# One of every five attention transposes moves from the DMA queue to TensorE

## The chip, the cores and the metric

The kernel runs on one core of a Trainium2 chip. Its time is the device time in microseconds (us) of one execution. Before the change the median of three runs was 1784.25 us (1779.7 to 1787.0). An engine here is one of TensorE (PE in the profile, with its weight loads as PEld), VectorE (DVE), ScalarE (ACT), GpSimd (POOL) and SyncE (SP), which only issues transfers.

## The reference

The program computes an attention with a position bias and feeds it to a mixture of eight experts whose gate is balanced by eight rounds of row and column normalisation. Batch 4, 8 heads, 576 positions, head size 64; 2304 tokens, model width 512, hidden width 1024.

```
scores = q @ k.T / sqrt(64) + bias            # 4 x 8 x 576 x 576
attn   = exp(scores - max);  attn /= sum + 1e-9
x      = (attn @ v), heads side by side       # 2304 x 512
P      = exp(x @ w_gate - max), 8 x (rows to 1, columns to 1, times N/E)
out    = sum over 8 experts e of P[:, e] * (relu(x @ w1[e]) @ w2[e])
```

## The kernel before

Every fp32 matrix is held as a pair of fp16 matrices, a high part and a low remainder, and products are formed from such pairs.

**The attention** works in 16 units, one for each pair of heads of each batch (`units`, line 687). The 576 queries of one head are cut into tiles of 128 rows: four full ones, and a half tile of 64; the half tiles of the two heads of a unit share the fifth tile. A unit has five steps (`unit_steps`, line 1086): for `gi` 0 and 1, one step per head with two tiles each, and for `gi` 2 one step with the fifth tile alone. A tile passes through these stages: `st_scores` (PE, into a PSUM tile `s`), `st_max` (DVE, adds the bias and takes the maximum, gives `sb`), `st_exp` (ACT), `st_rcp` (DVE), `st_hi` (ACT writes the high half of the probabilities into `ah`), `st_lo` (DVE writes the low half). `ah` has two buffers, and holds 2 x 576 numbers for each tile of a step. The probabilities must then be transposed so that the keys lie on the partitions: nine blocks of 128 x 128 for one tile (4.5 high, 4.5 low), eighteen for a step with two tiles. Line 975 does it with one transposing DMA on the SP queue, from `ah` to `aT` (three buffers for eighteen blocks; the fifth tile has one buffer of its own, `aT4`, printed as aT in the trace). Two steps later `attend` (line 977) multiplies `aT` with the values on PE, into PSUM tile `pv`, and `fin` writes the result as a high and a low half.

The same stretch of time also holds other work. The first 130 us or so compute the bias. All units load q, k, v and bias tiles (`nat`, `bt`) on the same SP queue, and split and transpose q and k: `u_trans` (line 753) transposes 18 blocks of `qk` on PE with `id16` as the moving operand, into a PSUM tile `l1`, from which ACT copies eight and two blocks and DVE eight. The first expert's products (`run_piece`, line 870, PSUM tiles `l1` and `l2`) are filled in between at lower priority.

The PSUM tile `s` has two buffers of 1024 fp32 columns each, that is two banks of 2048 bytes per partition. `ps_s` (line 449) hands them out in turn.

**What sets the order.** The instructions are not issued as they are written. `Plan` (line 43) collects them with their operands, finds what depends on what, and lays them out by a list scheduling with assumed costs (`cost`, `transfer`); each engine then runs its own list strictly in that order. So a new instruction can shift all that follows it in the attention. The experts 1 to 7 come after a first `plan.emit` (line 1185), in a plan of their own.

Of the kernel before, what the change touches and what calls it, by code (L numbers as in the profile page):

```python
# [9 lines left out]
F16 = mybir.dt.float16  # L10
# [8 lines left out]
P = 128  # L19
# [251 lines left out]
def attention_sinkhorn_moe(ctx, tc, q, k, v, w1, b1, w2, wg, m1, m2, xm, xm4, xf, sel, out):  # L271
# [11 lines left out]
    plan = Plan()  # L283
    vec, act, pool, pe, sync = (
        Engine(plan, e, n)
        for e, n in ((nc.vector, "dve"), (nc.scalar, "act"), (nc.gpsimd, "pool"), (nc.tensor, "pe"), (nc.sync, "dma"))
    )
# [15 lines left out]
    id16 = consts.tile([P, P], F16, name="id16")  # L303
# [109 lines left out]
    with ExitStack() as actx:  # L413
# [35 lines left out]
        def ps_s():  # L449
            return psA.tile([P, 1024], F32, name="ps_s", tag="s", bufs=2)  # L450
# [68 lines left out]
        for kind in range(1, 4):  # L519
            vec.scalar_tensor_tensor(  # L520
                out=wr,
# [8 lines left out]
            out=wa.rearrange("p g (j k) -> p (g j) k", j=4),  # L530
# [92 lines left out]
        def bias_step(between=()):  # L623
# [27 lines left out]
            out=w1r, in0=pw[:, H : H + 2], scalar1=s_wb[:, 0:1], scalar2=2.0**-11, op0=ALU.mult, op1=ALU.mult  # L651
# [5 lines left out]
            out=w2m,  # L657
# [22 lines left out]
        for i in range(2):  # L680
            r = slice(32 * i, 32 * i + 1)
# [113 lines left out]
        for n in range(8):  # L795
            for m in (2 * n, 2 * n + 1):
                nm, _, i = qk_order[m]
# [9 lines left out]
        with plan.urgent():  # L807
# [6 lines left out]
            out=c8, in0=u_qk[:, 0:1], scalar=0.125, in1=u_qk[:, 1:2], op0=ALU.mult, op1=ALU.mult  # L814
# [7 lines left out]
            out=g, in0=g0, scalar=s_qk[:, 0:1], in1=s_qk[:, 1:2], op0=ALU.mult, op1=ALU.mult  # L822
# [140 lines left out]
        def st_lo(s):  # L963
            n, ah = len(s["sb"]), s["ah"]
            s["aT"] = wrk.tile([P, 9 * n, P], F16, name="aT", tag="aT" if n == 2 else "aT4", bufs=3 if n == 2 else 1)
            for i, sb in enumerate(s["sb"]):
                vec.scalar_tensor_tensor(
                    out=ah[:, i, S:],
                    in0=sb,
                    scalar=s["st"][:, 3, i : i + 1],  # L970
                    in1=ah[:, i, 0:S],
                    op0=ALU.mult,
                    op1=ALU.subtract,
                )
            sync.dma_start_transpose(out=s["aT"], in_=ah.rearrange("p n s -> p (n s)"))

        def attend(u, gi, ss):

# [158 lines left out]
        for n in range(NS + LAG + 1):  # L1137
# [19 lines left out]
            if 0 < n <= NS:  # L1157
                s = steps[n - 1]
                st_hi(s)
                st_lo(s)  # L1160
                u, gi, hh = s["key"]
                groups.setdefault((u, gi), []).append(s)
                if gi == 2 or hh == 1:
                    due.append((n + LAG, u, gi, groups.pop((u, gi))))
# [21 lines left out]
        vec, act, pool, pe, sync = nc.vector, nc.scalar, nc.gpsimd, nc.tensor, nc.sync  # L1186
# [682 lines left out]
    for n, (e, b) in enumerate(seq):  # L1869
        r = visit[n]  # L1870
        i, at_end, leaves = (b, r % 2), n % 5 == 4, visit[n + 1 : n + 2] != [r]
# [96 lines left out]
```

## Time and profile before

| | us |
|---|---|
| median of 3 runs (range) | 1784.25 (1779.7 to 1787.0) |
| the profiled execution | 1784.56 |
| its span in the trace | 1782.8 |
| around the span | 1.76 |
| attention units with five steps each, steady stretch | 258 to 488 |
| last attention products | about 516.7 |

The profiled execution is 0.31 us above the median. Line L210 is the helper in which every planned instruction is recorded, so the attention is read by the names of the tiles. `l` stands for the PSUM tiles l1 and l2, `id` for the identity matrix, `area` for a large SBUF area that holds the first expert's weights at that time, `xc` and `xb` for the attention's output. The share of the DMA engines is the mean over the core's 16 engines.

How the views below are read. A row of the windows has the stretch and its length, then the busy time of PE, PEld, DVE, ACT and POOL with the number of instructions, then TensorE's granted clock (1.00 is its upper level), the share of the DMA engines and GB/s. A row of the waits says who waited for whom, and then the total in us, how often, and the longest. A row of the timeline has the start, the duration, the engine, the line, the operation and how many instructions were merged; the merged span begins with the first and ends with the last. A row of the chain has the start and the length of one piece. A group of instructions has its number, then the busy time of all in us and the mean duration of one in ns (instructions that overlap count once in the busy time), and then the idle time of its engine just before and who ended it.

### The profile page before, as it was taken

The numbers are of one execution on the slowest core, as the hardware profiler recorded it, in microseconds if no ns is written. First come the engines' busy times: TensorE is split into PE (matmuls) and PEld (weight loads), VectorE is DVE, ScalarE is ACT, GpSimd is POOL, SyncE is SP. The second block draws the span as 40 slices with busy tenths as digits, with TensorE's granted clock in tenths as the row PEclk, the third lists the DMA queues.
The fourth block names the chain that finished last, engine by engine and source line by source line (L and its number), as shares of the span: only waits on it lengthen the run. The fifth ranks groups of instructions, "written<-read, shape, count | busy, mean of one in ns | idle before, by whom it ended". The sixth has DMA issues, their size and how long they took to land.

```text
span 1782.8 us, 40479 instructions
## 1 busy us (share of the span) xinstructions
PE 1686.8 (95%) x16640; PEld 1377.4 (77%) x16640; DVE 1447.8 (81%) x2627; ACT 1086.3 (61%) x1930; POOL 78.7 (4%) x90
## 2 busy tenths in 40 slices
PE   7887897898989999999999999999999999999998
PEld 4544564555666688888988898889888988898887
DVE  6898988898968898778887787878788878876666
ACT  7887888888856675545564555565555544453443
POOL 0120012122200000000000000000000000000000
PEclk9988799999999999999999999999999999999999
DMA  7769999999993164644473557445545653463321
GB/s 259 240 160 225 206 196 200 200 201 194 202 268 136 68 204 181 231 165 163 170 279 135 201 190 248 154 143 213 214 173 180 237 192 131 160 238 103 104 73 37
DMA packets 303358, 324.24 MB, mean 182 GB/s; under 512 B 191420, under 2 KB 231876, under 8 KB 298180
## 3 DMA queue, kind: packets, MB, share of 16 engines
q1 hardware_dynamic: 303172, 321.65, 60.0%
q8 instruction: 130, 2.13, 0.5%
q14 instruction: 56, 0.46, 0.1%
HBM read 189.86 MB, written 88.08 MB: 156 GB/s over the span
## 4 chain that ended last, share of the span: by engine, by line
PE 78%; DVE 8%; DMA 7%; ACT 3%; issue 2%; SPq 0%; DVEq 0%; ACTq 0%
PE bankA L1591 18%; PE bankA L1611 13%; PE bankE L1591 9%; PE bankE L1611 9%; PE bankB L1611 9%; PE l L210 6%; PE bankB L1591 4%; DMA aT<-ah 4%; PE s L210 4%; PE pv L210 3%; ACT area L210 2%; DVE ah L210 1%; DVE area L210 1%; DVE sb L210 1%; PE bankS L1427 1%
## 5 line engine op out<-in xcount | busy, mean ns | idle before, releaser
L1591 PEld LDWEIGHTS <-slot 128*128 128x128 f16 x5040 | 450.7, 98 | 48.3 <-issue 2.5
L1611 PEld LDWEIGHTS <-hA 128*128 128x128 f16 x2268 | 222.4, 98 | 27.1 <-issue 0.6
L210 PEld LDWEIGHTS <-area 128*128 128x128 f16 (+1 forms) x2477 | 155.2, 101 | 101.5 <-issue 33.2
L1591 PE MATMUL bankA<-xt,slot 128*128 128x256 f16 (+1 forms) x1680 | 186.1, 262 | 0.2 <-ACT u L1648 0.2
L1591 PE MATMUL bankE<-xt,slot 128*128 128x256 f16 (+1 forms) x1680 | 186.1, 262 | 0.0
L1636 ACT ACTIVATE hA<-c 128x512 f16<-128x512 f32 x189 | 118.0, 627 | 111.3 <-DVE c L1214 110.4
L1611 PEld LDWEIGHTS <-hS 128*128 128x128 f16 x1512 | 147.2, 98 | 22.2 <-ACT hS L1636 3.0
L1611 PEld LDWEIGHTS <-area 128*128 128x128 f16 x1512 | 148.0, 98 | 18.5 <-issue 1.4
L210 DVE SCALAR_TENSOR_TENSOR ah<-sb,st,ah 128x576 f16<-128x576 f32 x144 | 122.4, 876 | 24.1 <-ACT ah L210 23.9
L1214 DVE SCALAR_TENSOR_TENSOR hA<-c,hA 128x512 f16<-128x512 f32 x189 | 127.5, 685 | 12.3 <-ACT hA L1636 10.2
L1695 ACT COPY u<-bankA 128x512 f32<-128x512 f32 (+1 forms) x70 | 37.8, 540 | 157.6 <-PE bankA L1611 157.4
L210 ACT ACTIVATE ah<-sb,st 128x576 f16<-128x576 f32 x144 | 106.2, 770 | 37.6 <-DMA aT<-ah 33.5
L1648 ACT ACTIVATE u<-bankA 128x512 f32<-128x512 f32 x126 | 75.1, 596 | 67.6 <-PE bankA L1591 63.8
L210 ACT ACTIVATE sb<-sb,st 128x576 f32<-128x576 f32 x144 | 110.4, 769 | 7.4 <-DVE st L210 7.1
L210 PE MATMUL l<-area 128*128 128x512 f16 (+1 forms) x413 | 110.6, 385 | 3.5 <-ACT ys L210 0.4
L1214 DVE SCALAR_TENSOR_TENSOR acc<-c,fs,acc 128x256 f32<-128x256 f32 x252 | 110.6, 480 | 2.1 <-DMA out_dram<-acc 0.2
L210 PE MATMUL s<-qkT 128*128 128x512 f16 (+3 forms) x560 | 84.5, 302 | 23.0 <-DVE st L210 22.1
L1611 PE MATMUL bankA<-area,hS 128*128 128x256 f16 x756 | 88.6, 273 | 3.2 <-ACT hS L1636 2.5
L1611 PE MATMUL bankA<-area,hA 128*128 128x256 f16 x756 | 89.8, 276 | 0.0
L1611 PE MATMUL bankA<-area 128*128 128x256 f16 x756 | 88.2, 273 | 1.0 <-ACT u L1695 1.0
L1611 PE MATMUL bankE<-area,hS 128*128 128x256 f16 x756 | 88.5, 273 | 0.0
L1611 PE MATMUL bankB<-area,hA 128*128 128x256 f16 x756 | 88.2, 273 | 0.0
(239 smaller groups left out, 3155.6 us busy)
## 6 DMA issues: line engine op xcount, KB each, us to landing
sc_w<-stage SPq DMA_DIRECT2D x84, 512.0 KB
acc<-sc_y SPq DMA_DIRECT2D x102, 256.0 KB
area<-sc_w SPq DMA_DIRECT2D x48, 512.0 KB
sc_y<-acc SPq DMA_DIRECT2D x84, 256.0 KB
xt<-sc_t SPq DMA_DIRECT2D x18, 1024.0 KB
slot<-sc_w SPq DMA_DIRECT2D x36, 512.0 KB
bt<-sc_bias SPq DMA_DIRECT2D x26, 576.0 KB
raw<-in_moe_w_dram SPq DMA_DIRECT2D x28, 512.0 KB
```

The lines of the kernel that those rows point to most:

```text
L210: self.plan.record(self.name, cost, lambda: fn(*args, **kw), ins, outs, move)
L1214: vec.scalar_tensor_tensor(out=o, in0=x, scalar=s, in1=y, op0=op0, op1=op1)
L1427: pe.matmul(r, id16 if sg > 0 else nid16, v[:, a, 2 * dq : 2 * dq + 2, tok * w : tok * w + w], start=(j == 0), stop=(j == len(seq_) - 1),)
L1591: pe.matmul(ps[:, jf * w : jf * w + w], t[:, a, c * 512 + f * P : c * 512 + f * P + P], x(xp, c), start=(first and jf == 0 and c == 0 and ...
L1611: pe.matmul(ps[:, j * 256 : j * 256 + 256], h[:, a, fc * w + j * P : fc * w + j * P + P], t[:, wp, fc * 256 : fc * 256 + 256], start=(firs ...
L1636: on_act(0.58, lambda: act.activation(h[:, 0, sl], x, AF.Relu if relu else AF.Copy), [r], wk)
L1648: on_act(0.55, lambda: act.activation(tmp[k], bank[b], f, scale=HS), [b], [k], 0)
L1695: on_act(0.27 * nt, lambda: act.copy(tmp[k][:, :n], bank[b][:, :n]), [b], [k], 0)
```

## The change

For the step with the fifth tile (`gi` 2) no transposing DMA is issued any more. Instead a tile of the `s` ring is taken, read as fp16, and nine blocks of `ah` are transposed into it on PE, as one piece for the planner. ACT then copies blocks 0 to 4 (640 columns) to `aT4`, DVE blocks 5 to 8 (512 columns). The other four steps of a unit keep their DMA.

```
@@ -972,7 +972,17 @@  st_lo
-            sync.dma_start_transpose(out=s["aT"], in_=ah.rearrange("p n s -> p (n s)"))
+            u, gi, hh = s["key"]
+            if not (gi == 2):
+                sync.dma_start_transpose(out=s["aT"], in_=ah.rearrange("p n s -> p (n s)"))
+                return
+            for i in range(n):
+                ps = ps_s().bitcast(F16)[:, : 9 * P].rearrange("p (r x) -> p r x", x=P)
+                with plan.as_one():
+                    for r in range(9):
+                        pe.transpose(ps[:, r], ah[:, i, r * P : (r + 1) * P], id16)
+                act.copy(s["aT"][:, 9 * i : 9 * i + 5], ps[:, :5])
+                vec.tensor_copy(s["aT"][:, 9 * i + 5 : 9 * i + 9], ps[:, 5:])
```

In all 16 transfers go, and 144 block transposes, 16 copies of ACT and 16 of DVE come. Apart from the lines of the source, the lists of all engines are the same from the end of the attention on. Within it the planner lays out everything after the first fifth tile anew.

On the SP queue, near the end of the attention, the order before is this (the number before the bracket is the shape; `DMAHW` are completion counters of earlier transfers):

```order
L210 DMA bt_1_123<-sc_bias_70 128x1152 [waits DMAHW6_49,DVE_49]
L210 DMA_TRANSPOSE aT_1_124<-ah_1_144 128x18x128 [waits DMAHW7_49,DVE_49,PE_49]
L210 DMA_TRANSPOSE aT_2_138<-ah_0_142 128x18x128 [waits DMAHW0_49,DVE_49,PE_49]
L210 DMA_TRANSPOSE aT_0_122<-ah_1_144 128x18x128 [waits DMAHW1_49,DMAHW5_49,DVE_49,PE_49]
L210 DMA_TRANSPOSE aT4_0_117<-ah_0_142 128x9x128 [waits DMAHW2_49,DVE_49]
L210 DMA_TRANSPOSE aT_1_124<-ah_1_144 128x18x128 [waits DMAHW3_49,DMAHW7_49,DVE_49,PE_49]
```

And now, in the same place:

```order
L210 DMA_TRANSPOSE aT_0_122<-ah_0_142 128x18x128 [waits DMAHW1_49,DVE_49,PE_49]
L210 DMA_TRANSPOSE aT_1_124<-ah_1_144 128x18x128 [waits DMAHW0_49,DMAHW3_49,DVE_49,PE_49]
L210 DMA bt_1_123<-sc_bias_70 128x1152
L210 DMA_TRANSPOSE aT_2_138<-ah_0_142 128x18x128 [waits DMAHW2_49,DMAHW4_49,DVE_49,PE_49]
L210 DMA_TRANSPOSE aT_0_122<-ah_1_144 128x18x128 [waits DMAHW7_49,DVE_49,PE_49]
```

The nine-block transfer between the large ones is gone; the large ones now follow each other directly, with only loads between them.

On PE, in the thirteenth unit, the scores of one step end and the q and k blocks of a later unit follow. Before (`s_0` and `s_1` are the two buffers of the scores' PSUM tile):

```order
L210 LDWEIGHTS qkT_1_129
L210 MATMUL s_1_118<-qkT_1_129 128x512 [waits DVE_49]
...
L210 MATMUL s_1_118<-qkT_1_129 128x64
L210 LDWEIGHTS qk_0_125
L210 MATMUL l1_1_115<-id16_68,qk_0_125 128x128 [waits DVE_49]
```

And now:

```order
L210 MATMUL s_1_118<-qkT_1_129 128x512 [waits DVE_49]
...
L210 LDWEIGHTS ah_0_142 [waits Activation_49]
L210 MATMUL s_0_116<-id16_68,ah_0_142 128x128
...
L210 LDWEIGHTS ah_0_142 [waits DVE_49]
...
L210 LDWEIGHTS qk_0_125
L210 MATMUL l1_1_115<-id16_68,qk_0_125 128x128 [waits DVE_49]
...
L210 MATMUL s_0_116<-qkT_1_129 128x512 [waits Activation_49]
```

Nine transposes stand between, four behind a wait for ACT's half of `ah` and five behind one for DVE's half; the next scores into `s_0` wait for ACT's copy.

On ACT the same place reads before as follows (`sb` in and out is `st_exp`, into `ah` is `st_hi`):

```order
L210 ACTIVATE sb_5_141,st_1_135<-sb_5_141,st_1_135 128x576
L210 ACTIVATE sb_0_133,st_1_135<-sb_0_133,st_1_135 128x576 [waits DVE_49]
L210 COPY qkT_0_126<-l1_0_113 128x1024 [waits PE_49,Pool_49]
L210 ACTIVATE ah_1_144<-sb_3_137,st_0_132 128x576 [waits DMAHW4_49,DVE_49]
L210 ACTIVATE ah_1_144<-sb_4_140,st_0_132 128x576
```

And now:

```order
L210 ACTIVATE sb_5_141,st_1_135<-sb_5_141,st_1_135 128x576
L210 ACTIVATE sb_0_133,st_1_135<-sb_0_133,st_1_135 128x576 [waits DVE_49]
L210 COPY aT4_0_117<-s_0_116 128x640 [waits DVE_49]
L210 ACTIVATE ah_1_144<-sb_3_137,st_0_132 128x576 [waits DMAHW2_49]
L210 ACTIVATE ah_1_144<-sb_4_140,st_0_132 128x576
L210 COPY qkT_0_126<-l1_0_113 128x1024 [waits Pool_49]
```

The new copy stands ahead of `st_hi` of the next step, and what it waits for is DVE's copy of the other four blocks. DVE's copy waits for PE's transposes, and ACT's for DVE's: the two do not run side by side. That is so in 12 of the 16 units; in the other four DVE's copy waits for ACT's.

## Rows read from the trace of the kernel before

**Rows 1.** The page: busy us, then PE and the DMA in 40 slices, tenths.

```profile
PE 1686.8 (95%) x16640; PEld 1377.4 (77%) x16640; DVE 1447.8 (81%) x2627; ACT 1086.3 (61%) x1930; POOL 78.7 (4%) x90
...
PE   7887897898989999999999999999999999999998
...
DMA  7769999999993164644473557445545653463321
```

**Rows 2.** Windows: a stretch of the attention, one of the experts.

```profile
258.00:488.00 230.00, 203.07 (x2027) 130.19 (x2025) 203.91 (x452) 192.04 (x389) 49.49 (x50) 0.97 0.96 200
700.00:1700.00 1000.00, 994.89 (x9557) 892.12 (x9555) 796.89 (x1294) 521.09 (x859) 0.00 (x0) 1.00 0.51 181
```

**Rows 3.** Waits, 186 to 509 us: the four that bear on this.

```profile
ACT ah L210 <- DMA aT<-ah: 26.2, 24, 2.2
DVE ah L210 <- ACT ah L210: 23.9, 23, 2.5
PE s L210 <- DVE st L210: 21.7, 27, 2.1
PE pv L210 <- DMA aT<-ah: 7.5, 9, 2.6
```

**Rows 4.** Chain of waits, 150 to 520 us, shares by line.

```profile
by line: PE l L210 25.1%; DMA aT<-ah 20.7%; PE pv L210 13.0%; PE s L210 9.2%; DVE ah L210 6.3%; issue 5.1%; DVE sb L210 3.8%; DVE area L210 2.4%; ACT ah L210 2.0%; DMA area<-in_moe_w_dram 1.5%; DVE sms L210 1.2%; DVE qk L210 1.2%; ACT sb L2
```

**Rows 5.** Timeline of the SP queue in one unit.

```profile
412.07 3.68 SPq L210 DMA_TRANSPOSE aT<-ah  x1
415.80 1.26 SPq L210 DMA_DIRECT2D nat<-in_q_dram  x2
417.17 3.28 SPq L210 DMA_TRANSPOSE aT<-ah  x1
420.54 0.53 SPq L210 DMA_DIRECT2D sc_y<-ys  x1
421.17 1.33 SPq L210 DMA_TRANSPOSE aT<-ah  x1
422.59 0.52 SPq L210 DMA_DIRECT2D bt<-sc_bias  x1
```

**Rows 6.** The same timeline: two nine-block transfers, four units apart.

```profile
258.01 1.25 SPq L210 DMA_TRANSPOSE aT<-ah  x1
...
351.11 1.39 SPq L210 DMA_TRANSPOSE aT<-ah  x1
```

**Rows 7.** Chain of waits, 409 to 425 us: one passage through a transpose.

```profile
414.97 2.20 PE l L210 x15
417.17 4.85 DMA aT<-ah
422.02 0.04 issue
422.06 1.93 PE pv L210 x27
```

**Rows 8.** Groups of instructions by form, 150 to 520 us.

```profile
L210 PE MATMUL l<-id,qk 128*128 128x128 f16 x216 | 18.1, 224 | 2.9 <-DVE area L210 1.8 <-ACT qkT L210 0.6 <-DVE qk L210 0.2
L210 ACT COPY qkT<-l 128x1024 f16<-128x1024 f16 x12 | 12.0, 1003 | 2.8 <-PE l L210 2.6 <-issue 0.2
L210 DVE COPY qkT<-l 128x1024 f16<-128x1024 f16 x12 | 8.2, 686 | 2.1 <-PE l L210 1.8
L210 ACT COPY qkT<-l 128x256 f16<-128x256 f16 x12 | 4.3, 358 | 0.9 <-PE l L210 0.9
```

**Rows 9.** Timeline: eight block transposes of TensorE in a row.

```profile
413.86 0.62 PE L210 MATMUL l<-id,qk 128*128 128x128 f16 x8
```

**Rows 10.** Waits in the tail of the attention, 486 to 512 us.

```profile
DVE ah L210 <- ACT ah L210: 7.1, 4, 2.5
ACT ah L210 <- DMA aT<-ah: 5.3, 4, 2.2
```

## The prediction

> **What bounds the kernel now.** I read the page first, for where the span goes. TensorE is busy 95% of it, and in the slices it is at 9 from the thirteenth on, but for the last; the DMA engines fill their slices from the fourth to the twelfth and not after [rows 1]. The windows say the same in numbers: from 700 to 1700 us PE is busy 994.89 of 1000 us with the DMA at 0.51, and that part keeps its order. So the change acts only on the attention, and what it wins or loses there moves the rest as a block.
>
> In the steady stretch of the attention, 258 to 488 us, four resources are nearly level: PE 203.07 of 230 us (88.3%), DVE 203.91 (88.7%), ACT 192.04 (83.5%), and the DMA engines at 0.96 [rows 2]. The fullest one is the DMA. The waits show how it is felt: ACT waits for a transfer out of `ah` to end (24 times, 26.2 us), because a buffer of `ah` is free only when its transpose has landed; DVE then waits for ACT's half of `ah` (23 times, 23.9 us); PE waits for `aT` itself only 7.5 us, and 21.7 us for DVE to release a scores tile [rows 3]. The chain of waits gives the weights: of 370 us, PE's three lines hold 47.3% (25.1 + 13.0 + 9.2), the transposing transfers 20.7%, that is 77 us, and DVE's named lines some 15% [rows 4]. One passage of the chain through an eighteen-block transfer takes 4.85 us, of which its 3.28 us on the queue are the larger part [rows 5, 7].
>
> **What goes.** Sixteen nine-block transfers. One holds the SP queue for 1.25 to 1.39 us, 1.33 in the middle; an eighteen-block one for 3.28 to 3.68 us, so that half of it, up to 1.85, is the other bound [rows 5, 6]. In all 21 to 30 us of a queue that is nearly always full, about 1.3 to 1.85 us in a unit. A unit is 23.3 us long (from the nine-block transfer at 258.01 us to the fourth one after it, at 351.11, divided by four [rows 6]), so the DMA's 0.96 would fall to about 0.89. What this frees is bounded by what is now waited for the transposes: 26.2 us (ACT) and 7.5 us (PE), 33.7 together [rows 3]. Below, nothing may come back, since four eighteen-block transfers in each unit remain and each still has to land before its buffer is free; it could even cost, as the planner lays out all transfers anew and two large ones now stand next to each other on the queue. I take half of the 33.7, about 17, and of that nine tenths, since 23.9 of ACT's 26.2 us were handed on to DVE: 15 us. The tail speaks for a real share: from 486 to 512 us, where little else is left to do, ACT waits 5.3 us for transposes and DVE 7.1 us for ACT [rows 10].
>
> **What comes on PE.** 144 block transposes, nine in a unit. The same form exists for q and k: 216 of them keep PE busy 18.1 us, 84 ns each, though one alone lasts 224 ns, because they overlap [rows 8]; eight in a row end within 0.62 us [rows 9]. So 9 x 84 = 0.76 us in a unit, 12.1 us in all; at the other end, without any overlap, 9 x 224 = 2.0 us, 32 us in all. I take 12.1, since these too stand in a row. PE has idle time in the stretch, 27 of 230 us, and its work is on the chain for 47.3% of it; 12.1 x 0.47 = 5.7 us.
>
> The Trainium skill prices such a transpose higher: its page "TensorE: Matmul & The Clock Gate", section "Part 4: PE-mode transpose", gives about 390 ns alone and about 275 ns within a kernel. By 275 ns the 144 would be 40 us, and 40 x 0.47 = 19 us on the path. The rows above show 224 ns from start to end of one but 84 ns of engine time where several follow each other, so the trace disagrees with that price as a cost per transpose, and I don't use it.
>
> **What comes on ACT and DVE.** ACT copies 1024 columns in 1003 ns and 256 in 358 ns [rows 8], which makes 0.84 ns a column and 0.68 us for 640: 10.9 us in all. DVE copies 1024 columns in 686 ns [rows 8]; 512 take between half of it and all of it, 0.34 to 0.69 us, and I take 0.37, near the lower end, as the fixed part is small in ACT's two rows: 5.9 us in all. On the chain ACT's named lines hold some 3% and DVE's some 15% [rows 4], so 0.3 and 0.9 us. ACT's idle time covers its copy; if that cover goes, it is 10.9 us.
>
> **The new waits.** PE's transposes wait for ACT's and then for DVE's half of `ah`. Behind them in PE's strict order stand the blocks of q and k of a later unit and the first expert's products, which had no need to wait. DVE's copy waits for PE, ACT's copy for DVE's, and behind ACT's copy stands `st_hi` of the next step; and the next scores in that buffer wait for ACT's copy. The trace has no such wait. The nearest row is PE's wait for DVE before scores: 27 times, 21.7 us, 0.8 us each [rows 3]. Sixteen of that size are 12.9 us; nothing is the other end, since the planner puts 0.62 us of q and k blocks and first-expert products between the transposes and the scores that need the buffer back. I take a quarter, 3 us: most of what PE waits for here it would have waited for a little later. The released `ah` buffer cuts the other way, and lies in the 15 us.
>
> The Trainium skill has a rule on this: "PSUM — Partial Sum Buffer", section "PSUM bank collisions raise a hardware error", says that two engines must not touch one bank in the same partitions at a time, two readers included. Nine blocks are 2304 bytes, and the second copy starts in the first copy's bank, so the two copies take turns, as the order shows; no run here shows their time. Side by side they would take 0.68 us, in turn 1.05.
>
> **The sum.** Costs 5.7 + 0.3 + 0.9 + 3 = 9.9 us, gain 15 us: 5 us less. The profiled execution took 1784.56 us (span 1782.8 and 1.76 around it), 0.31 above the median, which I neglect: 1784.5 - 5 = 1779.5 us.
>
> **Rivals.**
> (A) The transfers are the pace, and their time comes back nearly whole. For it: 0.96 of the DMA engines, the chain's 77 us, the tail. Against: DVE and PE have only 26 and 27 of 230 us left, and get work added. Price: 21 us off, costs of 6.9 on (5.7, 0.3, 0.9, no new waits): 14 less, 1770 us; at the far end 30 off, and 1762.
> (B) The new ties between PE, DVE and ACT become the bound: all 12.1 us of transposes lie on the path and each unit has one more wait of 0.8 us at the transposes or at the scores behind them, 12.9 us; the gain of 15 stays. 25 - 15 = 10 more, 1795 us. It decides once a unit's new waits and PE work on the path exceed 15 / 16 = 0.94 us. For it: PE is on nearly half of the chain, and its 21.7 us of waits for DVE show how easily its order runs dry. Against: the planner has placed fill between. If the gain fails as well, 1809.
> (C) The blocks do not overlap here, and each costs its 224 ns: 32 us, 15 of them on the path, with 1.2 for the copies and 3 of waits 19, less 15: 4 more, 1789 us. Against it are the 84 ns of the same form. The skill's 275 ns on the page named above would make it 8 more, 1793 us.
> (D) The change does not do what it says, because the freed queue time is taken by loads that were behind and PE's work falls into its idle time: 1784 us. It has the same sign as my forecast within what can be measured, and is counted with it.
>
> **How the numbers follow.** Forecast with D 0.38, A 0.29, B 0.26, C 0.07. A measurement of this kernel can tell 0.5%, 9 us, from no change. Faster than 1775.5: most of A (0.28) and the lower edge of the forecast (0.07), 0.35. Slower than 1793: most of B (0.20) and a part of C and of the forecast's upper edge (0.05), 0.25. The rest is 0.40. The forecast alone would lie between 1772 and 1788; with A's 1762 and B's 1795 and a little beyond taken in, the range is 1763 to 1798.
>
> **What would show it.** In the profile after: 64 transposing transfers instead of 80; the DMA share in the steady stretch near 0.9; ACT's wait for transfers from `ah` down from 26.2 us towards 13, and DVE's for ACT with it; a group of transposes into `s` near 84 ns of busy time each, ACT's copy at 0.68 us and DVE's at 0.37; the first expert-gate matmul some 5 us earlier than before, and the same distance from there to the end. The sum is wrong if PE waits for `ah` or for ACT's copy in most units (B), if ACT's waits for transfers vanish altogether (A), or if the DMA share stays at 0.96 and the waits with it (D).

## The result, and the profile after

The changed kernel took 1800.98 us (median of 4 runs, 1797.24 to 1804.52) beside 1784.93 us (median of 4 runs, 1779.7 to 1787.0) of the kernel before: a ratio of 1.0086, 95% interval 1.0059 to 1.0113. It is slower by some 15 us, against a forecast of 5 us less and a range that ended at 1798. A second measurement of the same kernel (e4 below) gave 1.0059 (1.0047 to 1.0071). So the loss is 10 to 15 us, and both intervals lie above 1.

The profiled execution took 1801.62 us, its span is 1799.8. Of the page, busy times, then PE and the DMA in 40 slices, beside [rows 1]:

```profile
PE 1693.0 (94%) x16784; PEld 1383.7 (77%) x16784; DVE 1449.9 (81%) x2643; ACT 1096.7 (61%) x1946; POOL 79.5 (4%) x90
...
PE   7777897899999999999999999999999999999998
...
DMA  7769779898883254654474457345645653463321
```

PE has 144 instructions more and 6.2 us more busy time, and the span is 17 us longer. The windows, to be read against [rows 2]:

```profile
258.00:488.00 230.00, 201.42 (x2054) 129.87 (x2052) 199.90 (x447) 193.68 (x391) 48.75 (x50) 0.97 0.87 185
700.00:1700.00 1000.00, 989.81 (x9484) 885.58 (x9483) 794.56 (x1291) 520.03 (x857) 0.00 (x0) 1.00 0.52 181
```

In the attention's steady stretch the DMA share fell from 0.96 to 0.87, as predicted. But PE and DVE did not fill what became free: PE went from 203.07 to 201.42 and DVE from 203.91 to 199.90 of 230 us, with new work among it. All three compute engines and the DMA have idle time now, which says that the loss is waiting, not work. The gate's first product, which marks the end of the attention, shows where it arose; before, then after:

```profile
516.69 0.96 PE L1270 MATMUL bankS<-wgs,xa 128*128 128x8 f16 x32
```

```profile
526.22 0.93 PE L1280 MATMUL bankS<-wgs,xa 128*128 128x8 f16 x31
```

Before, the product began 9.5 us earlier. From there to the end of the span it is 1273.6 us, against 1266.1 before; this part has the same instructions in the same order in both kernels, and over all the profiles of this case it took from 1265.0 to 1273.6 without any link to what was edited. In e4, a second profile of the changed kernel, it took 1269.1 us, and the attention ended at 530.1. I count it as scatter of single executions, and go by the timed ratios where a few us matter.

The waits of the attention (186 to 525 us; who waited for whom, total us, times, longest), against [rows 3]:

```profile
PE s L210 <- DVE st L210: 22.0, 23, 2.4
DVE ah L210 <- ACT ah L210: 19.2, 21, 2.6
ACT ah L210 <- DMA aT<-ah: 12.9, 11, 2.2
DVE sb L210 <- PE s L210: 9.7, 15, 2.0
ACT aT L210 <- DVE aT L210: 9.4, 6, 3.6
ACT sb L210 <- DVE st L210: 6.3, 10, 1.3
PE l L210 <- DVE qk L210: 5.8, 4, 4.2
PE pv L210 <- DMA aT<-ah: 4.0, 5, 1.2
```

ACT's wait for transfers went from 26.2 to 12.9 us and PE's from 7.5 to 4.0. DVE's wait for ACT, which I had expected to follow, only fell from 23.9 to 19.2. Four rows are new or larger: ACT waits 9.4 us for DVE's copy, and 6.3 us for the row maxima, DVE waits 9.7 us for scores, and PE 5.8 us for the q and k blocks (0.2 before). The last of them does not go with the loss: it is 7.8 us in e3 below, which is not slower than before, and absent in e12, the slowest. Two of the others had these rows before:

```profile
DVE sb L210 <- PE s L210: 7.3, 12, 1.5
ACT sb L210 <- DVE st L210: 2.0, 4, 0.8
```

The chain by line, against [rows 4]:

```profile
by line: PE l L210 25.4%; DMA aT<-ah 13.0%; PE s L210 12.1%; PE pv L210 11.3%; DVE ah L210 8.0%; issue 6.9%; DVE sb L210 6.6%; ACT ah L210 2.2%; DVE qk L210 1.9%; DMA area<-in_moe_w_dram 1.7%; DVE area L210 1.6%; DVE st L210 1.4%; DVE sms L
```

The transfers went from 20.7% to 13.0%, and in their place came the scores (9.2 to 12.1%), DVE's two lines (6.3 to 8.0, 3.8 to 6.6) and issue. The new work itself, busy us and mean ns, then the idle time of its engine ahead of it, against the sizes that I took from [rows 8]:

```profile
L210 PE MATMUL s<-id,ah 128*128 128x128 f16 x144 | 11.9, 225 | 2.7 <-DVE ah L210 2.0 <-ACT ah L210 0.5
L210 ACT COPY aT<-s 128x640 f16<-128x640 f16 x16 | 11.0, 689 | 12.0 <-DVE aT L210 9.4 <-PE s L210 2.3
L210 DVE COPY aT<-s 128x512 f16<-128x512 f16 x16 | 6.8, 424 | 5.0 <-PE s L210 3.4 <-ACT aT L210 1.6
```

The durations were near the forecast: 83 ns of engine time for a transpose (84), 689 ns for ACT's copy (680), 424 for DVE's (370). So the size of the work itself does not explain the miss. The timeline of one unit shows what its place did (start, duration, instruction, idle time before it in brackets):

```profile
222.09 1.33 DVE L210 SCALAR_TENSOR_TENSOR ah<-sb,st,ah 128x576 f16<-128x576 f32 x1
223.29 0.68 PE L210 MATMUL s<-id,ah 128*128 128x128 f16 x9
223.35 1.76 DVE L210 SCALAR_TENSOR_TENSOR vs<-nat,sms,vs 128x640 f16<-128x640 f32 x1
...
225.83 0.41 DVE L210 COPY aT<-s 128x512 f16<-128x512 f16 x1
226.28 0.69 ACT L210 COPY aT<-s 128x640 f16<-128x640 f16 x1 [3.64 <-DVE aT L210]
```

ACT stood still from 222.64 us. PE's nine blocks, which needed DVE's half of `ah`, were ready at 223.97. DVE then had 1.9 us of other work ahead of its copy in its list, its copy ran from 225.83, and ACT's copy, which is placed behind DVE's, came 3.64 us late. It is the worst of the six.

### The profile page after: what moved, and what is told of

Same layout as the page of the kernel before. It is cut to its first block, busy times and chain, and to the rows that moved or that the text cites. A ratio compares the mean times of both kernels' runs of the same rounds, so it can differ in the third digit from the quotient of the medians.

```text
span 1799.8 us, 40708 instructions
## 1 busy us (share of the span) xinstructions
PE 1693.0 (94%) x16784; PEld 1383.7 (77%) x16784; DVE 1449.9 (81%) x2643; ACT 1096.7 (61%) x1946; POOL 79.5 (4%) x90
## 4 chain that ended last, share of the span: by engine, by line
PE 75%; DVE 10%; DMA 8%; ACT 3%; issue 3%; SPq 0%; DVEq 0%; ACTq 0%
PE bankA L1601 17%; PE bankA L1621 13%; PE bankE L1601 8%; PE bankE L1621 8%; PE bankB L1621 8%; PE l L210 6%; PE bankB L1601 4%; PE s L210 4%; PE pv L210 3%; DMA aT<-ah 3%; DVE ah L210 2%; DVE sb L210 2%; ACT area L210 1%; DMA xc<-in_moe_w_dram 1%; DVE area L210 1%
## 5 line engine op out<-in xcount | busy, mean ns | idle before, releaser
L1621 PEld LDWEIGHTS <-area 128*128 128x128 f16 x1512 | 148.1, 98 | 19.3 <-issue 2.0
L1224 DVE SCALAR_TENSOR_TENSOR hA<-c,hA 128x512 f16<-128x512 f32 x189 | 127.6, 686 | 13.2 <-ACT hA L1646 11.2
L210 DVE SCALAR_TENSOR_TENSOR ah<-sb,st,ah 128x576 f16<-128x576 f32 x144 | 120.5, 860 | 19.4 <-ACT ah L210 19.2
L1621 PE MATMUL bankB<-area 128*128 128x256 f16 x756 | 88.2, 273 | 0.0
```

Of the source, the lines that this page charges most:

```text
L210: self.plan.record(self.name, cost, lambda: fn(*args, **kw), ins, outs, move)
L1224: vec.scalar_tensor_tensor(out=o, in0=x, scalar=s, in1=y, op0=op0, op1=op1)
L1621: pe.matmul(ps[:, j * 256 : j * 256 + 256], h[:, a, fc * w + j * P : fc * w + j * P + P], t[:, wp, fc * 256 : fc * 256 + 256], start=(firs ...
```

## The experiments

In all of them the time is given as the ratio to the kernel before on the same chip, and "us" is that ratio less 1, times 1785. "Planned anew" means that the planner laid out the edited list by itself.

| run | what it is | ratio (95%) | us |
|---|---|---|---|
| e1 | changed, blocks 5 to 8 in another PSUM tile | 1.0129 (1.0114 to 1.0145) | +23.0 |
| e2 | changed, ACT copies all nine | 1.0108 (1.0093 to 1.0124) | +19.3 |
| e3 | no transposes, no transfers, planned anew | 0.9984 (0.9971 to 0.9997) | -2.9 |
| e4 | the changed kernel again | 1.0059 (1.0047 to 1.0071) | +10.5 |
| e5 | before's order, the 16 transfers left out | 0.9968 (0.9953 to 0.9984) | -5.7 |
| e6 | changed kernel's order, its work left out | 1.0048 (1.0030 to 1.0066) | +8.6 |
| e7 | the same with PE's transposes | 1.0052 (1.0031 to 1.0072) | +9.3 |
| e8 | the same with the 16 transfers instead | 1.0077 (1.0056 to 1.0097) | +13.7 |
| e9 | before, one unused turn of the scores' pair per unit | 1.0017 (1.0001 to 1.0034) | +3.0 |
| e10 | changed, with such a turn | 1.0086 (1.0068 to 1.0105) | +15.4 |
| e11 | e2 with such a turn | 1.0113 (1.0092 to 1.0133) | +20.2 |
| e12 | changed, transposes in the l1 tiles | 1.0167 (1.0147 to 1.0188) | +29.8 |
| e13 | before's order, all the work in it, through pv | 1.0070 (1.0051 to 1.0089) | +12.5 |
| e14 | before, one assumed cost 0.155 for 0.165 | 1.0037 (1.0021 to 1.0053) | +6.6 |
| e15 | before, the same cost 0.175 | 1.0047 (1.0029 to 1.0065) | +8.4 |
| e16 | changed, the same cost 0.155 | 1.0081 (1.0063 to 1.0099) | +14.5 |
| e18 | e13, DVE alone copies | 1.0042 (1.0024 to 1.0060) | +7.5 |
| e19 | e13, ACT alone copies | 1.0070 (1.0051 to 1.0089) | +12.5 |

**First: copies, work or order?** The expectations number three theories: 1, the two copies wait for each other; 2, PE's work; 3, the planner's new order.

e1 sends the second copy's blocks to an `l1` tile (which the first expert's products also use: in some units a part of its hidden values is overwritten):

```
+                p2 = ps_l1().bitcast(F16)[:, : 4 * P].rearrange("p (r x) -> p r x", x=P)
-                        pe.transpose(ps[:, r], ah[:, i, r * P : (r + 1) * P], id16)
+                        pe.transpose(ps[:, r] if r < 5 else p2[:, r - 5], ah[:, i, r * P : (r + 1) * P], id16)
-                vec.tensor_copy(s["aT"][:, 9 * i + 5 : 9 * i + 9], ps[:, 5:])
+                vec.tensor_copy(s["aT"][:, 9 * i + 5 : 9 * i + 9], p2)
```

> Blocks 5 to 8 go into a second PSUM tile (from the l1 ring), so that ACT's and DVE's copies no longer wait for each other. Theory 1 (the two copies taking turns hold ACT's queue: 9.4 us of waits of ACT for DVE's copy in the profile after): the time falls by 6 to 12 us, to about 1790, and ACT's wait for DVE's copy is gone. Theory 2 (PE's added work and its waits for ah are the price): within 4 us of the changed kernel, about 1800. Theory 3 (the planner's new layout and the freed DMA do it): not settled by this run, 1790 to 1800.

e2 gives both copies to ACT:

```
-                act.copy(s["aT"][:, 9 * i : 9 * i + 5], ps[:, :5])
-                vec.tensor_copy(s["aT"][:, 9 * i + 5 : 9 * i + 9], ps[:, 5:])
+                act.copy(s["aT"][:, 9 * i : 9 * i + 9], ps)
```

> ACT alone copies all nine blocks, about 1.1 us a unit; DVE copies none. Theory 1: ACT no longer stands behind DVE's queue, 1788 to 1794 us in spite of 0.4 us more ACT work a unit. Theory 2: about 1800. Theory 3: 1790 to 1800, as the layout changes again.

e3 leaves the fifth tile's transposition out altogether (`aT4` holds zeros), and the planner lays out what is left:

```
-            sync.dma_start_transpose(out=s["aT"], in_=ah.rearrange("p n s -> p (n s)"))
+            u, gi, hh = s["key"]
+            if gi == 2:
+                if u == 0:
+                    pool.memset(s["aT"], 0.0)
+                return
+            sync.dma_start_transpose(out=s["aT"], in_=ah.rearrange("p n s -> p (n s)"))
```

> The fifth tile is transposed by nobody: no transfer, no PE work, no copies; aT4 is set to zero once, so the output of the last 64 queries of each head is left out. This is the freed DMA alone. The forecast's gain of 15 us (half of the waits for transfers): about 1770 us. If the transfers were the pace (A): 1760 to 1765. If freeing the DMA is worth nothing in the end because other waits take its place: 1780 to 1788.

e4 is the changed kernel, unedited.

> The changed kernel again, for a second profile. In the first one the attention ended 9.5 us later than before and the expert layers, whose order is unchanged, took 7.5 us more. If that second part belongs to the change, it comes again, 1797 to 1804 us with 6 to 8 us of it in the experts; if it was that execution's own, it is 0 to 4 us and the time is near 1795.

Each of the first two takes away the wait of ACT for DVE's copy, and both were slower than the changed kernel. Each edit also changed the planner's order, and this confounds them: they do not say what the copies' turn costs. Nor did the time come out where any of the three theories had put it: 1809 and 1806 us are above all their ranges. e3 bounds the matter from below: with the work and the transfers gone and a new order, 2.9 us are gained, which is the case of a freed DMA that is worth little in the end.

**Then: order and work apart.** The next four let the planner work with the same list as one of the two kernels, and then leave instructions out when they are issued, so that the order of everything else stays. The expectations call it theory W that the added work is the price, and theory L that the new layout (the planner's order) is. `mute` empties the last planned entry:

```
+        def mute(fn=None):
+            n = plan.nodes[-1]
+            plan.nodes[-1] = (*n[:2], fn or (lambda: None), *n[3:])
```

e5 mutes the nine-block transfers in the kernel before (`aT4` holds zeros):

> The kernel before with its order kept word for word (the planner still counts the sixteen nine-block transfers), but the transfers themselves left out; aT4 is set to zero once, so the output of the last 64 queries of each head is left out. This is the freed DMA with no new layout. Theory W (the added work is the price, freeing the DMA is worth little): as the run with nobody transposing, 1781 to 1787 us. Theory L (the freed DMA is worth the forecast's 15 us, but the planner's new layout gives it back): 1770 to 1776 us.

e6 mutes transposes and copies in the changed kernel:

> The changed kernel with its order kept, but the 144 block transposes and both copies left out (fifth tile transposed by nobody, aT4 zero; the last 64 queries of each head are left out). Against the run with before's order kept it shows the layout alone. Theory W: the layout costs nothing, 1781 to 1787 us, and the 12 to 15 us up to the changed kernel are the work's. Theory L: the layout is the loss, 1793 to 1799 us.

e7 mutes the copies only:

> The changed kernel's order, with the block transposes on PE but without the two copies (aT4 zero; the last 64 queries of each head are left out). Theory W split in two: if PE's work and its waits for ah are the price, 1793 to 1799 us; if the copies are (ACT standing 9 to 10 us behind DVE's copy), 1785 to 1789. Theory L: as the layout alone, 1793 to 1799.

e8 mutes the work and issues the nine-block transfer in the place of the copies:

> The changed kernel's order on PE, ACT and DVE, but the fifth tile is transposed by its nine-block DMA as before, issued at the place of DVE's copy; no PE transposes, no copies. Theory W: the layout alone costs nothing, so this is the kernel before, 1783 to 1791 us. Theory L: 1795 to 1805 us, all of the loss with none of the work.

The freed transfers are worth 5.7 us in the order of before (e5) and 5.2 in the changed one (e8 against e6, where the transfer stands at the later place of DVE's copy). PE's transposes cost 0.7 there, nothing that can be told (e7 against e6). The copies cost the rest, between e7 and the two measurements of the changed kernel: 1 to 6 us. Each of the last three is uncertain by some 5 us. But e6 against e5, two kernels with the same work, differ by 14.3 us (uncertain by some 4). That is the new order, and with it one thing more that e6 keeps: the turn that the transposes' tile takes in the scores' pair of PSUM buffers, of which below. So theory L has the loss right, but not its premise that the freed transfers are worth 15 us. The ends of the attention in the single profiles agree in the main: 509.7 us in e5, 520.6 in e6, 525.2 in e7 and 526.2 and 530.1 in the two profiles of the changed kernel. The waits in the attention, e5 first, then e6:

```profile
PE s L210 <- DVE st L210: 19.1, 26, 2.1
DVE sb L210 <- PE s L210: 5.9, 13, 1.5
ACT sb L210 <- DVE st L210: 1.9, 4, 0.8
```

```profile
PE s L210 <- DVE st L210: 25.8, 23, 2.4
DVE sb L210 <- PE s L210: 14.9, 20, 1.8
ACT sb L210 <- DVE st L210: 8.7, 17, 1.5
PE l L210 <- DVE qk L210: 5.2, 3, 4.0
```

Every link of the chain from scores to maxima to exponentials runs dry for longer in the second, and the last two more often. In the steady stretch (as in [rows 2]), e5 then e6:

```profile
258.00:488.00 230.00, 208.70 (x2078) 133.17 (x2077) 207.67 (x461) 197.64 (x400) 49.47 (x50) 0.96 0.90 189
```

```profile
258.00:488.00 230.00, 200.63 (x1996) 128.29 (x1994) 200.41 (x444) 189.50 (x382) 47.55 (x50) 0.95 0.88 186
```

With identical work to do, PE is busy 208.70 of 230 us in the one and 200.63 in the other.

**Is it the scores' pair of buffers?** The transposes take a turn in the two-buffer PSUM pair `s`. After an odd number of turns the next scores get the buffer that the last ones hold, and must wait for DVE. Counted in PE's instruction list, two scores in succession share a buffer 3 times of 144 before, 39 times now. Theory R says that this is the cost. e9 adds to the kernel before only a turn, which nothing uses:

```
+            if s["key"][1] == 2:
+                ps_s()
```

> The kernel before, all its transfers kept, no transpose on TensorE and no copy; the one edit is that each unit takes one buffer of the two-buffer PSUM pair of the scores and leaves it unused, so that the two score tiles on either side of it land in the same buffer (18 such pairs of neighbours counted in TensorE's order, 3 in the kernel before). Theory R (the turn taken in the scores' pair of buffers is the cost): slower than the kernel before by 4 to 9 us, with VectorE waiting longer for the scores and TensorE longer for the row maxima in attention. Rival (the cost is the new order of the other instructions, whatever the buffers): within 2 us of the kernel before.

e10 adds the line `ps_s()` ahead of the transposes' tile in the changed kernel, and e11 does so in e2:

> The changed kernel with one unused buffer taken from the scores' pair ahead of the transposes' tile, so that the pair is turned twice and fewer neighbouring scores share a buffer (29 pairs of neighbours against 39 in the changed kernel). Theory R: faster than the changed kernel by 2 to 6 us (1792 to 1797 us beside a kernel before of 1785). Rival (order): as the changed kernel within 2 us.

> As the run before, with ScalarE copying all nine blocks (29 pairs against 44 in the earlier run with ScalarE alone, which took 1806 us). Theory R: 1794 to 1800 us, that is 6 us or more below that earlier run. Rival (order): 1803 to 1808 us.

e12 transposes into two `l1` tiles instead, and first closes a pair of the first expert's products that is open:

```
-                ps = ps_s().bitcast(F16)[:, : 9 * P].rearrange("p (r x) -> p r x", x=P)
+            flush(0)
+            t5, t4 = (ps_l1().bitcast(F16)[:, : w * P].rearrange("p (r x) -> p r x", x=P) for w in (5, 4))
...
+            act.copy(s["aT"][:, :5], t5)
+            vec.tensor_copy(s["aT"][:, 5:9], t4)
```

> The changed kernel with the transposes written into two tiles of another PSUM ring (five blocks and four, each copied by its own engine), so that the scores' pair is not touched: 3 pairs of neighbours in one buffer, as in the kernel before. The work is that of the changed kernel. Theory R: the loss is gone, 1781 to 1789 us beside a kernel before of 1785, and the wait of VectorE for the scores in attention is back near 6 us. Rival (the work or the order costs): 1796 us or more.

As the whole cause the theory fell. A turn alone cost 3.0 us, below the 4 to 9 that it asked for, though the interval (0.2 to 6.1) reaches into them; fewer neighbours in one buffer gained nothing in e10 and e11; and e12, which leaves the pair alone, was the slowest of all. In e12's waits the signature of the pair is indeed gone (DVE's wait for scores was 9.7 after and 7.3 before), but the time is not back:

```profile
DVE sb L210 <- PE s L210: 6.3, 14, 1.0
ACT sb L210 <- DVE st L210: 5.9, 10, 1.0
```

What e12 loses in the `l1` tiles, where the products of the first expert and the q and k blocks live, was not followed up; PE's wait for DVE ahead of products into `l` stands out, at 10.1 us (2.8 before, 0.4 in the changed kernel).

As a part of the cost the pair is not excluded. Where two scores share a buffer, PE can stand still until DVE has read the scores just before. In e6 it does, here for 2.04 us:

```profile
206.97 0.81 DVE L210 CUSTOM_DVE_ANT_0 sb<-s,br,sms 128x576 f32<-128x576 f32 x1
207.84 0.65 PE L210 MATMUL s<-xc 128*128 128x512 f16 x4 [2.04 <-DVE st L210]
```

Setting each tile's scores against DVE's reading of the tile before, I find 11 such waits in e6, 14.0 us in all, 12 in the changed kernel (9.8 us), 6 in e10 (6.8 us), and none in the kernel before, in e5, or in e9, e12, e14 and e15. PE's waits for the reading of the tile two before became shorter in all at the same time (23.7 us in e5, 19.8 in e6). So e9 has a turn but not this wait, and does not price it; e12, e14 and e15 lose time without it; and no run parts the order of e6 from its turn.

**The order by itself, and the work by itself.** e14 and e15 are the kernel before with one number of the planner nudged, the duration that it assumes for one block of a transposing transfer; e16 does the same in the changed kernel:

```
-            return 0.65, 0.165 * out.free_size() / P, 0.92
+            return 0.65, 0.155 * out.free_size() / P, 0.92
```

> The kernel before, all its work and transfers and PSUM turns; the one edit is the duration that the planner assumes for a transposed block in a transfer, 0.155 us for 0.165, which moves 45 of ScalarE's and 470 of TensorE's instructions in the list. Theory O (any order laid out anew loses against this one): slower than the kernel before by 1 to 6 us. Theories R and W: within 2 us of the kernel before, as often below as above.

> As the run before, with 0.175 us for 0.165, which moves more: 117 of ScalarE's and 1118 of TensorE's instructions, about as many as the change does (98 and 1083). Theory O: slower than the kernel before by 5 to 12 us. Theories R and W: within 2 us of the kernel before.

> The changed kernel with all its work, and 0.155 us for 0.165 in the planner (49 of ScalarE's and 458 of TensorE's instructions move against the changed kernel). Theory O: anywhere from 1788 to 1806 us, off the changed kernel by 2 us or more to either side. Theory W (the work, not the order): within 2 us of the changed kernel, 1797 to 1803 us.

e13 keeps the order of before on every engine and puts the work into it. When the muted transfer comes up, the nine transposes are issued, and 0.9 us of planned time later the copies; PSUM tile `pv` is taken, between two products that use it:

```
+                def work():
+                    for r in (8, 0, 1, 2, 3, 4, 5, 6, 7):
+                        nc.tensor.transpose(pv[:, r % 8], ah[:, 0, r * P : (r + 1) * P], id16)
+                    plan.late.append((plan.now + 0.9, copies))
+                def copies():
+                    nc.scalar.copy(aT[:, :5], pv[:, :5])
+                    nc.vector.tensor_copy(aT[:, 5:9], pv[:, 4:8])
```

> The order of the kernel before on every engine, word for word, with the 16 nine-block transfers left out and in their place nine transposes on TensorE, ScalarE's copy of 640 columns and VectorE's of 512, as in the changed kernel; the transposes go into the PSUM tile pv, between two products that use it, and not into the scores' pair. The tile holds eight blocks, so one of the nine is overwritten: the output of the fifth tiles is not the reference's. Theory O (the order laid out anew is what the changed kernel loses): as the kernel before or faster, 1779 to 1787 us beside 1785. Theory W (the work and its waits cost, more than the freed transfers give): 1792 us or more. Theory R (the scores' pair alone): as theory O here.

Both halves of the question came out against a single cause. A new order costs by itself: nothing but the order differs in e14 and e15, and they lost 6.6 and 8.4 us (theory O, that the order is the loss, asked for 1 to 6 and 5 to 12; theory W, that the work is, for less than 2). e16, the same nudge in the changed kernel, moved nothing that can be told: 14.5 us beside 10.5 and 15.4. Theory O had asked for a shift of 2 us or more there, so not every new order costs. The same row of the waits, ACT's for the maxima, grew in e14 and e15 as in the changed kernel; e14, then e15:

```profile
DVE sb L210 <- PE s L210: 10.1, 11, 1.8
ACT sb L210 <- DVE st L210: 6.8, 9, 2.2
```

```profile
ACT sb L210 <- DVE st L210: 11.1, 18, 1.3
DVE sb L210 <- PE s L210: 6.8, 12, 1.5
```

ACT's wait for the maxima was 2.0 us before. It is 1.7 to 2.7 in all five profiles that have the order of before (before, e5, e13, e18, e19) and 3.9 to 11.6 in all that have another order. It does not rise with the loss (3.9 in e3 with 2.9 us gained, 4.3 in e8 with 13.7 lost, 11.1 in e15 with 8.4 lost): it marks another order and does not price it. But the work in the kept order was not free either: e13 lost 12.5 us, at 1798 us, where theory O had 1779 to 1787 us and theory W 1792 or more. Its groups:

```profile
L1008 PE MATMUL pv<-id,ah 128*128 128x128 f16 x144 | 11.1, 224 | 0.9 <-DVE ah L236 0.5 <-DVE xa L236 0.3
L1012 ACT COPY aT<-pv 128x640 f16<-128x640 f16 x16 | 11.0, 689 | 7.8 <-PE pv L1008 7.7
L1013 DVE COPY aT<-pv 128x512 f16<-128x512 f16 x16 | 6.8, 425 | 20.4 <-ACT aT L1012 20.4
```

DVE stood idle for 20.4 us ahead of its 16 copies, each time until ACT's copy out of the same tile had ended. The last two runs let one engine copy alone (eight blocks; the ninth is left out). e18 has `nc.vector.tensor_copy(aT[:, :8], pv)` for the two copies, e19 `nc.scalar.copy(aT[:, :8], pv)`:

> The kept order with the transposes into pv, as two runs before, and one copy of VectorE alone (eight blocks, 1024 columns; the ninth is left out) in place of ScalarE's and VectorE's. If the turn that the two copies take is the cost of the work (theory T): VectorE's 18.4 us of idle time ahead of its copies falls below 6, and the time to 1781 to 1789 us beside a kernel before of 1786. If the work itself costs (PE's transposes, the sharing of pv, VectorE's longer copy): 1794 us or more.

> As the run before, with ScalarE alone copying the eight blocks. Theory T: 1781 to 1790 us, some more than with VectorE, since ScalarE's copy of 1024 columns is the longer one (1.0 us against 0.69). Work: 1794 us or more.

Their copies:

```profile
L1014 DVE COPY aT<-pv 128x1024 f16<-128x1024 f16 x16 | 11.0, 688 | 7.3 <-PE pv L1010 7.1
```

```profile
L1014 ACT COPY aT<-pv 128x1024 f16<-128x1024 f16 x16 | 16.1, 1009 | 8.0 <-PE pv L1010 8.0
```

Theory T, that the two copies' taking turns is the cost, holds for a part at most. Without the turn DVE's idle time went from 20.4 to 7.3 us (the theory asked for less than 6) and 5 us were gained, uncertain by as much, but with ACT alone nothing; both times, 1796 and 1800 us, lie where the rival, the work itself, had them. Set against e5, which is the same order without the work, the three fit another reading: 18.2, 13.2 and 18.2 us more for copies that, one after the other, take 17.8 (11.0 + 6.8), 11.0 and 16.1 us. Each difference is uncertain by some 4 us. So in an order that has no room for them the work costs about as much as its copies are long, whichever engine does them. That it is the copies is argued from these lengths and not shown: all three runs have PE's transposes too, which no run takes away in this order. That the sharing of `pv` has a part in it is not excluded either: PE's waits for the copies ahead of products into `pv` were 9.4 us in e13, 4.5 in e18 and 9.8 in e19.

## Why the prediction was wrong

- **Sizes of the work: right in the main.** 83 ns, 689 ns, 424 ns (DVE's copy, 15% over the 370), 64 transfers, a DMA share of 0.87 (0.89 forecast), ACT's waits for transfers at 12.9 us (13).
- **The gain, 15 us: wrong, it is 5 to 6** (e5, and e8 against e6). The step that failed here is the one from ACT's and PE's waits to the time: half of the 33.7 us and nine tenths of that. In e5 those waits fell by 14.7 us (to 14.9 and 4.1), nearly as much as forecast, and 5.7 reached the end. DVE's wait for ACT, which was to carry the gain on, fell by 5.0 only, from 23.9 to 18.9.
- **PE's transposes, 5.7 us on the path: too much, as far as can be told.** In the changed kernel's order they cost 0.7 us, uncertain by some 5. The price of some 275 ns a block, from the Trainium skill's page "TensorE: Matmul & The Clock Gate", section "Part 4: PE-mode transpose", does not hold here as a cost per transpose: the 144 blocks kept the engine busy for 11.9 us, not 40.
- **ACT's and DVE's copies, 1.2 us: too little.** I weighted them by the share of their engines on the chain, and so took them as hidden. In the order of before the work, transposes and copies together, cost 13 to 18 us, about the copies' whole length; in the order that the planner made for them the copies cost 1 to 6. I had named the price of lost cover (10.9 us for ACT) and given it no weight.
- **The new waits, 3 us: the step that failed most.** It was known that the planner lays out anew everything after the first fifth tile, but the sum has waits at the new instructions alone, and no term for the order of all the others. That order, with its turns of the scores' pair, costs 14 us with none of the new instructions in it (e6 against e5). This is the largest term. The wait that the prediction did name at the scores, for ACT's copy to free their buffer, is 0.3 us in the changed kernel.
- **The rivals.** B had the right side, and 1795 us for 1797 to 1801, but its number is in good part luck: it kept the gain of 15 us and put all 12.1 us of transposes on the path, two errors that nearly cancel. Its other half, one more wait per unit of 12.9 us in all at the transposes or the scores behind them, is nearer to the runs. ACT's wait for DVE's copy, 9.4 us in 6 of 16 units, is a wait of this kind; e1 and e2, which take it away, did not get faster, but they were planned anew. PE's 12 waits at scores that share a buffer (9.8 us) are of this kind too, though they are for DVE's reading and not for the new copies. A, C and D fall: the transfers' time did not come back, the blocks do overlap, and the time did change.

The sum by the runs: 5.7 gained, 14.3 lost by the order with its turns of the pair, 0.7 by the transposes, 1 to 6 by the copies: 10.5 to 15.4 us. The terms add up because each is a difference of neighbouring runs; what is shown is their size in this sequence. They do not add in another one: work without a new order cost 13 to 18 us (e13, e18, e19 against e5), and a new order without the work 14, but the two together not 27 or more. The likely reason, argued from this and not tested, is that the new order is slacker and has the copies in it where they were planned.

Open is what makes the order of before the better one. Two nudges of one number and an added turn all lost against it (e9, e14, e15), and e3, planned anew, gained 2.9 where e5 gained 5.7 (intervals that overlap). Rows in which another order shows are named above; the instruction whose place decides is not, and the share of the scores' pair is open too. No version with the transposition done was faster than the kernel before.

## What to carry to other kernels

Where a planner lays out the instructions, an edit has two prices: its work, and the new order. Measure them apart: keep the order and leave the work out, and nudge one planner number without any edit, which shows how much the order alone can move the time (here 7 to 8 us in the kernel before, more than the gain that was forecast, and nothing that can be told in the changed one). And where three engines are each busy for over 80% of the time and wait for one another, put the full length of an added copy into the range as a bound, unless a gap of that length is seen at the place where it will stand.

## What was not expected of the hardware

- Two copies out of one PSUM tile, by ACT and by DVE, do not run side by side in this program, whose instructions wait for each other there: in e13 each of the 16 copies of DVE started when ACT's ended, so 1.11 us for both (0.689 + 0.424) and not 0.69. In the changed kernel none of the 16 pairs overlap either. Out of two PSUM tiles they do: in e1, 13 of the 16 pairs overlap, at unchanged durations, as here:

```profile
384.86 0.67 ACT L210 COPY aT<-s 128x640 f16<-128x640 f16 x1
384.88 0.42 DVE L210 COPY aT<-l 128x512 f16<-128x512 f16 x1 [0.27 <-PE l L210]
```

  The waits within one tile agree with the rule of the Trainium skill's page "PSUM — Partial Sum Buffer", section "PSUM bank collisions raise a hardware error", that two engines do not touch one bank at a time, two readers included.
- The part after the attention, the same instructions in the same order, took between 1265.0 and 1273.6 us in single profiled executions, so the span of one profile does not tell differences below some 8 us.
